# One-core chunk attention with a gated convolution: four single warming products, and the whole order of queues and buffers dealt anew

## The chip, the cores and the metric

The kernel runs on one NeuronCore of a Trainium2 chip. Five engines work side by side, each through its own queue in program order: TensorE (PE; its weight loads are listed as PEld), VectorE (DVE), ScalarE (ACT), GpSimd (POOL) and SyncE (SP), which here only issues DMAs. The metric is device microseconds of one execution; less is better. Before the change it is 277.35 us, the median of 3 runs (276.96 to 277.71).

## What is computed

```
scores = q @ k^T / 8 in chunks of 64 tokens;  attn = softmax(scores);  x = attn @ v      (8 batches x 8 heads x 576 x 64)
x as [8, 576, 512]:  gate = sigmoid(causal depthwise convolution of x with 5 taps);  val = x @ w_val
out = (gate * val) @ w_out
```

All of it is float32 for the caller. The kernel keeps that accuracy by splitting operands of the two large products in a high and a low part (`xh`, `xl`; `v_hi`, `v_lo`; `gh`, `gl`; `o_hi`, `o_lo`), so that each large product is three products of TensorE's faster 32-bit form: high by high, high by low, low by high. The weights come as 64-bit words and are cut into the two parts on the chip.

## The kernel before

The 4608 tokens are cut into nine groups of 512 (g = 0 to 8), each group's 512 channels into two halves (p = 0, 1). For a half there is a chain of pieces, each a handful of instructions:

- `lq`, `lk`, `lv` load queries, keys and values (512 KB each; those of group 0 partly in halves of 256 KB); `lw v c` and `lw o c` load a unit c of the two weight matrices, `lc` the taps.
- `S g p b` are the scores of a half (64x64 products on PE); `mx` finds the row maximum (DVE); then either `ng` and `ea` (exponentials on ACT with the sum read out, 16 times two instructions) and `rc`, or `sb` (DVE), `ex` (ACT), `sm` (DVE); `nm` scales by 1/sum (POOL).
- `T` or `TW` transposes (PE), `ec` copies the transposed weights out (ACT), `A g p` is attn @ v (PE); `xr`, `xd` and `xc` cut x into its high part, its low part and a plain copy (ACT, DVE, ACT); `hc` and `hb` keep the last tokens for the next group's convolution (POOL).
- `V g m c` is a product with w_val: three matmuls of 128x512, or one where a fourth number names the term. `vc` copies the sum out. `k0`, `k`, `kk`, `kx` are the convolution's taps (mostly DVE), `sg` the sigmoid, `gs` the gating product, `gr` and `gd` the cut of the result.
- `P g t c` is a product with w_out, `oc` (or `o1`) copies the sum out, `st` (or `s1`) stores it.
- `w1` to `w9`, `wa`, `wb`, `Q v c` and `wc` cut weight unit c; `W n s` is a stretch of n products of 128x512 and s of 128x64 on zeros, whose result nobody reads.

What runs when is written by hand: the string `ORDER` lists some 1030 pieces, and the loop at the end of the kernel function calls them one after the other. Each engine keeps that order in its queue, SP too. A capital D or G at a piece's end puts it on DVE or POOL. Three more tables set the rest. `SLOTS` names for every new tile the SBUF buffer (`z`, 28 whole ones and 10 in the tile `ys`), the PSUM bank (`b`, four of them) or the score buffer (`e`) that it takes. A tile that takes a buffer waits until its former tile's last reader is done; where that reader is a store, until the store has landed. `BEHIND` ties a piece on POOL to another piece that must have ended. A DMA issued from SP also takes one of eight completion counters in turn, and so waits for the DMA eight places before it.

Every instruction is recorded through one helper, so the profile gives nearly all of them one line (L144) and the tiles tell them apart:

```
def run(fn, *args, **kwargs):
    made.append(tc.keep_in_program_order(fn(*args, **kwargs)))
```

In the trace `z` and `ys` are the buffers of all kinds, `b` the banks, `e_row` the scores after the exponential, `mx` and `rs` the row maxima and sums, and `in_q`, `in_k`, `in_v`, `in_moe_w_val` and `in_moe_w_out` the inputs.

Of the kernel before, what the change touches and what calls it, by code (L numbers as in the profile page):

```python
# [22 lines left out]
rc 0 1 1,w6D v 3,sm 0 0,nm 0 1 1,ec 0 1 0,TW 0 1 1,Q v 3,lw v 0,lv 0 1,lv 0 0,lw o 0,lk 1 1,lq 1 1,w5 v 0,wc v 2,ec 0 1 1,wc v 3,
nm 0 0,w1 v 0,w4 c 0,mx 1 0,sb 1 0,A 0 1 1,A 0 1 0,TW 0 0,w2 v 0,xr 0 1 1,xr 0 1 0,xc 0 1 0,ec 0 0,ex 1 0,xc 0 1 1,V 0 3 2 0,
V 0 2 2 0,V 0 3 2 1,V 0 2 3 1,V 0 3 3 1,A 0 0,w3 v 0,w3 o 0,w1 o 0,w7 c 0,xd 0 1 0,w4 v 0,w8D c 0,w7 v 0,w9,sm 1 0,w6D v 0,
xd 0 1 1,w8 v 0,nm 1 0,wa v 0,xr 0 0,S 1 1 1,S 1 1 0,V 0 3 3 0,V 0 3 0 0,V 0 3 0 1,V 0 3 1 1,V 0 2 0 0,V 0 2 0 1,V 0 3 1 0,
V 0 2 1 1,V 0 2 3 0,V 0 2 1 0,T 1 0,lw o 3,lk 2 0,lv 1 0,lq 2 0,lv 1 1,lk 3 0,lw o 2,xc 0 0,k0 0 3,k0 0 2,k0 0 0,k0 0 1,ec 1 0,
xd 0 0,mx 1 1,k 0 3 2,ng 1 1,k 0 2 1,wbD v 0,w1 o 3,k 0 3 4,k 0 1 2,k 0 2 3,k 0 0 1,V 0 1 2 2,V 0 0 1 2,V 0 0 0 2,V 0 3 1 2,
V 0 3 2 2,V 0 0 2 0,V 0 1 3 1,V 0 0 3 0,V 0 3 3 2,V 0 0 2 2,V 0 2 1 2,V 0 1 1 2,V 0 0 1 0,V 0 1 0 2,V 0 1 3 2,V 0 2 0 2,V 0 2 2 2,
V 0 1 0 0,V 0 0 3 2,V 0 0 1 1,V 0 1 0 1,A 1 0,ea 1 1,w2 o 0,xr 1 0,xc 1 0,k 0 1 4,w3 o 3,rc 1 1,k 0 1 1,hc 0 1,nm 1 1,w1G o 2,  # L30
S 2 0 0,S 2 0 1,mx 2 0,xd 1 0,sb 2 0,V 0 1 2 1,V 0 2 2 1,V 0 3 0 2,V 0 0 3 1,V 0 1 2 0,V 0 1 1 1,V 0 1 3 0,V 0 0 2 1,V 0 1 1 0,
V 0 0 0 1,V 0 2 3 2,V 0 0 0 0,T 1 1,V 1 3 0,V 1 3 1,w2 o 3,w5 o 0,k0 1 1,w2 o 2,vc 0 0,ec 1 1,ex 2 0,lq 3 0,lq 2 1,lk 2 1,lk 4 1,
lw o 1,lv 2 1,lk 4 0,lq 3 1,lq 4 0,lv 2 0,lk 3 1,k 0 3 3,k 0 0 4,w4 o 0,k 1 1 3,w7 o 0,sm 2 0,A 1 1,S 2 1 1,S 2 1 0,vc 0 1,xc 1 1,
xr 1 1,mx 2 1,xd 1 1,ng 2 1,w8 o 0,nm 2 0,V 1 0 1,V 1 2 0,V 1 0 0,V 1 2 1,V 1 3 3,T 2 0,V 1 2 2,V 1 0 2,V 1 2 3,V 1 1 0,V 1 1 2,
V 1 1 1,w6 o 0,k0 1 3,w5 o 3,ea 2 1,ec 2 0,w4 o 3,k 0 0 2,w3 o 2,k 0 0 3,k 0 3 1,w3 o 1,k 0 2 4,k0D 1 2,k 0 2 2,k 1 1 1,w7 o 3,
rc 2 1,k 0 1 3,S 3 0 1,S 3 0 0,A 2 0,V 1 3 2,V 1 0 3,V 1 1 3,w1G o 1,nm 2 1,w8 o 3,sg 0 1,w6 o 3,xr 2 0,vc 1 1,sg 0 0,mx 3 0,
sb 3 0,xd 2 0,k 1 1 4,w4 o 2,waD o 3,gs 0 0,gs 0 1,k 1 2 4,TW 2 1,V 2 0 1,V 2 1 0,V 2 1 1,ec 2 1,xc 2 0,vc 1 0,w2 o 1,S 4 0 0,
A 2 1,xr 2 1,ex 3 0,xd 2 1,S 3 1 0,S 4 0 1,S 3 1 1,V 2 0 0,V 2 1 2,V 2 1 3,V 2 0 2,V 2 0 3,mx 4 0,sm 3 0,hc 0 0,wa o 0,wb o 0,
# [32 lines left out]
P 4 2 3,P 5 1 0,P 5 2 1,P 4 1 0,P 4 2 1,P 5 2 2,P 5 3 3,P 5 3 0,P 5 0 2,P 4 2 2,P 5 3 1,P 5 0 0,P 5 2 0,P 5 0 1,P 5 1 1,gr 6 1,
# [12 lines left out]
    z="21 1 24 27 13 25 9 12 26 3 21 6 7 10 24 8 5 18 19 14 4 8 27 22 3 9 24 23 10 13 7 15 6 11 8 27 17 15 10 14 0 "  # L84
# [660 lines left out]
```

## Time and profile before

| what | value |
|---|---|
| median of 3 runs | 277.35 us (276.96 to 277.71) |
| the profiled execution | 277.89 us, its span 276.1 us (1.8 us lie around the span) |
| PE busy | 265.8 us, 96% of the span |
| DVE, ACT, POOL busy | 236.5, 192.7 and 60.2 us |
| chain that ended last | 83% PE, 10% DMA, 2% DVE, 2% SP |
| granted TensorE clock, mean | 0.998 |
| moved by DMA | 42.48 MB; stores begin at 86 us, the last loads land near 151 us |

A busy matmul is counted to its modelled end, and matmuls overlap: in a dense stretch a product of 128x512 starts every 0.233 us (nine of them in the 2.10 us from 75.80 to 77.90), though one alone is listed with about 0.39 us. What counts on PE are therefore the starts, and the idle time in brackets before an instruction. DMAs leave SP in order and are served nearly in order; the time to landing is counted from the issue.

### The profile page before, as it was taken

How to read it: one execution, taken by the hardware profiler on the slowest of the kernel's cores; microseconds unless marked ns; L12 is line 12 of the kernel's file. 1: busy time of each engine (PE TensorE's matmuls, PEld its weight loads, DVE VectorE, ACT ScalarE, POOL GpSimd, SP SyncE). 2: the span in 40 equal slices, each digit the busy share in tenths (PEclk: the TensorE clock that was granted, in tenths of full speed). 3: DMA queues.
4: the chain of work that ended last, by engine and by line, in shares of the span. 5: the costliest groups of instructions: out<-in, count | busy, mean ns of one | idle time of the engine just before them, and what ended most of it. 6: DMA issues, size and time to landing. Idle time of an engine off the chain costs nothing.

```text
span 276.1 us, 8074 instructions
## 1 busy us (share of the span) xinstructions
PE 265.8 (96%) x3490; PEld 212.8 (77%) x3490; DVE 236.5 (86%) x316; ACT 192.7 (70%) x360; POOL 60.2 (22%) x59
## 2 busy tenths in 40 slices
...
PEclk9999999999999999999999999999999999999999
...
GB/s 241 391 373 221 285 350 363 303 3 182 409 26 158 374 223 271 53 331 204 5 233 229 2 2 2 0 0 2 0 0 1 2 0 0 0 0 61 265 379 209
DMA packets 14755, 42.48 MB, mean 154 GB/s; under 512 B 1536, under 2 KB 1792, under 8 KB 14720
## 3 DMA queue, kind: packets, MB, share of 16 engines
...
## 4 chain that ended last, share of the span: by engine, by line
PE 83%; DMA 10%; DVE 2%; SPq 2%; issue 1%; ACT 0%; DVEq 0%
PE b L144 83%; DMA z<-in_k 5%; DMA out<-z 3%; DMA z<-in_q 2%; SPq L144 2%; DVE e_row L144 1%; DVE mx L144 1%; DVE z L144 1%; ACT z L144 0%; DVEq L144 0%; ACT e_row L144 0%
## 5 line engine op out<-in xcount | busy, mean ns | idle before, releaser
L144 PE MATMUL b<-z,v_hi 128*128 128x512 f32 x288 | 93.9, 399 | 0.1
L144 PE MATMUL b<-o_hi,z 128*128 128x512 f32 (+1 forms) x296 | 93.9, 391 | 0.0
L144 ACT COPY z<-b 128x1024 f32<-128x1024 f32 (+2 forms) x63 | 59.7, 969 | 31.8 <-PE b L144 29.0
L144 PEld LDWEIGHTS b<-o_hi,z 128*128 128x128 f32 x296 | 55.1, 188 | 12.9 <-ACT e_row L144 0.2
L144 PEld LDWEIGHTS b<-z,v_hi 128*128 128x128 f32 x288 | 53.8, 188 | 13.2 <-issue 0.2
L144 DVE SCALAR_TENSOR_TENSOR z<-z,cw,z 128x509 f32<-128x509 f32 (+3 forms) x80 | 56.2, 739 | 1.9 <-ACT z L144 1.8
L144 PE MATMUL b<-o_lo,z 128*128 128x512 f32 (+1 forms) x148 | 57.5, 388 | 0.0
L144 PE MATMUL b<-z,v_lo 128*128 128x512 f32 x144 | 56.2, 396 | 0.0
L144 POOL TENSOR_TENSOR z<-e_row,rs 128x1024 f32<-128x1024 f32 (+1 forms) x17 | 31.5, 1856 | 46.7 <-DVE rs L144 33.4
L144 POOL TENSOR_TENSOR z<-z,z 128x1024 fp32r<-128x1024 f32 (+2 forms) x8 | 14.7, 1843 | 118.3 <-ACT z L144 101.0
L144 PEld LDWEIGHTS b<-o_lo,z 128*128 128x128 f32 x148 | 27.8, 188 | 6.0
L144 ACT ACTIVATE z<-z 128x1024 f32<-128x1024 f32 (+3 forms) x26 | 21.4, 843 | 14.9 <-DVE z L144 14.4
L144 DVE SCALAR_TENSOR_TENSOR ys<-ys,cw 128x509 f32<-128x509 f32 (+7 forms) x32 | 31.0, 1010 | 1.0 <-ACT ys L144 0.9
L144 PEld LDWEIGHTS b<-z,v_lo 128*128 128x128 f32 x144 | 27.0, 188 | 6.0
L144 DVE TENSOR_TENSOR z<-z,z 128x1024 f32<-128x1024 f32 (+2 forms) x22 | 25.4, 1170 | 5.1 <-ACT z L144 5.0
L144 ACT ACTIVATE e_row<-b,mx 128x64 f32<-128x64 f32 x80 | 23.8, 362 | 3.0 <-DVE mx L144 3.0
L144 DVE TENSOR_TENSOR z<-b,z 128x1024 fp32r<-128x1024 f32 (+1 forms) x19 | 21.7, 1161 | 2.3 <-ACT z L144 1.1
L144 DVE TENSOR_REDUCE mx<-b 128x16 f32<-128x1024 f32 (+1 forms) x19 | 21.7, 1142 | 1.9 <-PE b L144 1.9
L144 PEld LDWEIGHTS b<-z,z 64*64 64x64 f32 x1024 | 16.6, 135 | 8.2 <-issue 5.0
L144 PE MATMUL b<-z,z 64*64 64x64 f32 x1024 | 18.5, 221 | 4.4 <-DMA z<-in_k 3.9
L144 ACT CAST z<-b 128x1024 fp32r<-128x1024 f32 (+1 forms) x19 | 18.2, 976 | 6.1 <-PE b L144 6.0
L144 ACT ACTIVATION_READ_ACCUMULATOR e_row<-b,mx 128x1 f32 x80 | 20.3, 256 | 0.0
...
## 6 DMA issues: line engine op xcount, KB each, us to landing
out<-z SPq DMA_DIRECT2D x16, 512.0 KB, 5.1
z<-in_k SPq DMA_DIRECT2D x9, 512.0 KB, 4.4
z<-in_v SPq DMA_DIRECT2D x9, 512.0 KB, 7.9
ys<-in_v SPq DMA_DIRECT2D x9, 512.0 KB, 6.2
z<-in_q SPq DMA_DIRECT2D x8, 512.0 KB, 6.1
ys<-in_q SPq DMA_DIRECT2D x8, 512.0 KB, 7.7
ys<-in_k SPq DMA_DIRECT2D x7, 512.0 KB, 5.5
z<-in_moe_w_val SPq DMA_DIRECT2D x4, 512.0 KB, 5.2
```

The lines of the kernel that those rows point to most:

```text
L144: made.append(tc.keep_in_program_order(fn(*args, **kwargs)))
```

## The change

`ORDER` has the same 1030 pieces and four more: `W 1 1`, `W 1 3`, `W 1 4` and `W 1 2`, together 4 products of 128x512 and 10 of 128x64. The stretch `W 3`, which opened PE's queue, moves to a place between the scores of group 0, and `W 1 1` opens it. Everything else in `ORDER`, all buffer and bank numbers, and the ties of POOL (24 before, 27 now) are written anew. No function changes, and no other instruction is added or removed. At the front, `lv 0 1` is now issued ahead of `lw v 0`. One stretch of the diff, where the first result of the group 0 goes out (the rest of the table reads alike):

```
-V 3 0 2,V 3 1 2,V 3 0 0,V 3 3 0,P 0 1 3,V 3 1 1,V 3 3 3,V 3 3 2,V 3 2 2,V 3 2 1,V 3 3 1,ea 5 1,sg 1 0,oc 0 0,sg 1 1,gs 1 0,
+P 0 0 1,P 0 1 2,P 0 0 2,V 3 2 2,V 3 1 0,V 3 0 3,V 3 3 0,V 3 2 3,V 3 1 3,V 3 3 2,V 3 0 2,V 3 1 1,ea 5 1,oc 0 0,sg 1 0,sg 1 1,
```

The first place is PE's queue at the front, from the second weight unit's sum (three products into bank 3) to the third's. Before, the scores of group 1 (`b0_293`, 32 products) follow the first transposes (`b2_288`):

```order
L144 MATMUL b0_207<-z6_181,z21_179 64x64 x32
L144 MATMUL b3_279<-z12_102,ident_62 128x512
L144 MATMUL b3_279<-v_hi_67,signed_63 128x512
L144 MATMUL b3_279<-z26_109,signed_63 128x512
L144 MATMUL b2_288<-ident_62,z8_283 128x128 x4
L144 MATMUL b0_293<-z24_252,z10_250 64x64 x32
L144 MATMUL b2_288<-ident_62,z8_283 128x128 x4
L144 MATMUL b1_339<-z3_111,ident_62 128x512
```

And now, the same stretch of PE's queue without the products before the weight unit's sum:

```order
L146 MATMUL b3_283<-z10_104,ident_62 128x512
L146 MATMUL b3_283<-v_hi_67,signed_63 128x512
L146 MATMUL b3_283<-z16_109,signed_63 128x512
L146 MATMUL b2_300<-ident_62,z24_287 128x128 x4
L146 LDWEIGHTS warm_64
L146 MATMUL b1_305<-warm_64 128x512
L146 LDWEIGHTS warm_64
L146 MATMUL b1_305<-warm_64 128x64
L146 LDWEIGHTS warm_64
L146 MATMUL b1_305<-warm_64 128x64
L146 MATMUL b0_309<-z17_247,z11_245 64x64 x32
L146 MATMUL b2_300<-ident_62,z24_287 128x128 x4
```

`W 1 2` now stands between the first transposes and the scores of group 1, and takes bank 1, which the scores of group 0's other half had.

The second place is SP's queue around the first stores. Before, one store (`st 0 1`) stands there, and the values of group 4's half 0 (`lv 4 0`, into `z11_1662`) follow it directly in a buffer that a weight unit had:

```order
L144 DMA z14_1659<-in_q 128x1024
L144 DMA out_0<-z25_1522 128x2x512
L144 DMA z11_1662<-in_v 128x1024
L144 DMA ys_61<-in_k 128x1024
L144 DMA ys_61<-in_v 128x1024
L144 DMA ys_61<-in_q 128x1024
```

And now, the same stretch of SP's queue:

```order
L146 DMA z15_1676<-in_q 128x1024
L146 DMA out_0<-z16_1545 128x2x512
L146 DMA ys_61<-in_k 128x1024
L146 DMA ys_61<-in_v 128x1024
L146 DMA ys_61<-in_k 128x1024 x2
L146 DMA out_0<-z11_1667 128x2x512
L146 DMA z11_1684<-in_v 128x1024
L146 DMA ys_61<-in_q 128x1024
```

A second store (`st 0 0`, out of `z11_1667`, the tile that `oc 0 0` fills) now stands ahead of `lv 4 0`, and `lv 4 0` goes into the same buffer 11.

The third place is SP's queue at its last loads, those of values for groups 6 to 8. Before, `lv 6 1` (`z9_1972`) stands ahead of three stores of groups 0 and 2:

```order
L144 DMA ys_61<-in_q 128x1024
L144 DMA z9_1972<-in_v 128x1024
L144 DMA ys_61<-in_v 128x1024
L144 DMA out_0<-z17_2381 128x2x512
L144 DMA out_0<-z27_1652 128x2x512
L144 DMA z26_2395<-in_v 128x1024
L144 DMA ys_61<-in_v 128x1024
L144 DMA out_0<-z14_2170 128x2x512
```

And now, the same stretch of SP's queue:

```order
L146 DMA out_0<-z14_2188 128x2x512
L146 DMA ys_61<-in_v 128x1024 x2
L146 DMA out_0<-z16_2297 128x2x512
L146 DMA out_0<-z6_1973 128x2x512
L146 DMA z6_2410<-in_v 128x1024
L146 DMA ys_61<-in_v 128x1024
L146 DMA z20_2413<-in_v 128x1024
```

`lv 6 1` (`z6_2410`) now stands behind three stores, `st 2 0`, `st 2 1` (out of `z16_2297`, which `oc 2 1` fills) and `st 1 0` (out of `z6_1973`), and goes into the buffer of the last of them.

## Rows read from the trace of the kernel before

**Rows 1.** The page: busy time of each engine; PE's granted clock in 40 slices

```profile
PE 265.8 (96%) x3490; PEld 212.8 (77%) x3490; DVE 236.5 (86%) x316; ACT 192.7 (70%) x360; POOL 60.2 (22%) x59
...
PEclk9999999999999999999999999999999999999999
```

**Rows 2.** Timeline of PE at the front: start, length, instruction [idle before, releaser]

```profile
9.63 1.46 PE L144 MATMUL b<-z,z 64*64 64x64 f32 x64 [1.33 <-DMA z<-in_k]
...
11.74 0.69 PE L144 MATMUL b<-z,z 64*64 64x64 f32 x32 [0.65 <-DMA z<-in_k]
...
22.25 1.09 PE L144 MATMUL b<-ident,z 128*128 128x128 f32 x8 [0.64 <-POOL z L144]
26.06 1.16 PE L144 MATMUL b<-z,z 64*64 64x64 f32 x64 [0.45 <-DMA z<-in_q]
```

**Rows 3.** Timeline of PE from 143 to 158 us: its last waits on DVE

```profile
153.55 0.71 PE L144 MATMUL b<-ident,z 64*128 64x64 f32 x16 [0.22 <-DVE z L144]
...
154.69 0.72 PE L144 MATMUL b<-ident,ys 64*128 64x64 f32 x16 [0.42 <-DVE z L144]
```

**Rows 4.** Two stretches: length; PE, PEld, DVE, ACT, POOL; clock, DMA share, GB/s

```profile
12.00:22.00 10.00, 7.54 (x207) 5.13 (x197) 8.92 (x18) 9.04 (x39) 5.03 (x4) 1.00 0.97 374
80.00:100.00 20.00, 20.00 (x233) 16.38 (x232) 19.38 (x28) 17.81 (x48) 4.48 (x3) 1.00 0.55 191
```

**Rows 5.** Timeline of PE around one and around two groups of 64 small products

```profile
75.80 0.63 PE L144 MATMUL b<-o_hi,z 128*128 128x512 f32 x2
...
77.90 0.40 PE L144 MATMUL b<-o_hi,z 128*128 128x512 f32 x1
...
79.66 0.39 PE L144 MATMUL b<-o_lo,z 128*128 128x512 f32 x1
...
146.55 0.39 PE L144 MATMUL b<-z,v_hi 128*128 128x512 f32 x1
...
149.23 0.39 PE L144 MATMUL b<-z,v_lo 128*128 128x512 f32 x1
```

**Rows 6.** Timeline of DVE and ACT at the front

```profile
14.21 1.17 DVE L144 TENSOR_REDUCE mx<-b 128x16 f32<-128x1024 f32 x1
...
18.62 0.67 ACT L144 ACTIVATE z<-z 128x512 f32<-128x512 uint32 x1 [0.41 <-DMA z<-in_moe_w_val]
```

**Rows 7.** DMA issued at 11.5 us: KB each, median us to landing

```profile
z<-in_moe_w_val SPq DMA_DIRECT2D x1, 512.0 KB, 7.1
```

**Rows 8.** DMA queues from 13 to 16 us: packets, MB, share of 16 engines

```profile
q8 instruction: 1, 0.02, 2.3%
```

**Rows 9.** Timeline of DVE from 82 to 92 us

```profile
82.02 1.22 DVE L144 TENSOR_TENSOR z<-b,z 128x1024 fp32r<-128x1024 f32 x1 [0.48 <-ACT z L144]
83.16 2.72 DVE L144 SCALAR_TENSOR_TENSOR z<-z,cw,z 128x511 f32<-128x511 f32 x4
...
91.42 0.17 DVE L144 TENSOR_SCALAR mx<-mx 128x16 f32<-128x16 f32 x1
```

**Rows 10.** Timeline of ACT from 91 to 97 us: first and last of 32 instructions

```profile
91.62 0.31 ACT L144 ACTIVATE e_row<-b,mx 128x64 f32<-128x64 f32 x1 [2.04 <-DVE mx L144]
...
96.17 0.29 ACT L144 ACTIVATION_READ_ACCUMULATOR e_row<-b,mx 128x1 f32 x1
```

**Rows 11.** Timeline of ACT from 138 to 141 us: the copy ahead of a store

```profile
139.07 1.00 ACT L144 COPY z<-b 128x1024 f32<-128x1024 f32 x1
```

**Rows 12.** DMA issued at 253.39 us, with no other in flight: KB, us to landing

```profile
out<-z SPq DMA_DIRECT2D x1, 512.0 KB, 3.0
```

**Rows 13.** DMA issued at 98.37 us, with no other in flight

```profile
z<-in_k SPq DMA_DIRECT2D x1, 512.0 KB, 3.3
```

**Rows 14.** Timeline of PE: 16 transposes, then A 4 0

```profile
102.46 0.71 PE L144 MATMUL b<-ident,z 64*128 64x64 f32 x16
103.10 1.16 PE L144 MATMUL b<-z,z 64*64 64x64 f32 x64
```

**Rows 15.** DMAs issued at 140.09 and 140.54 us, behind a load

```profile
out<-z SPq DMA_DIRECT2D x2, 512.0 KB, 5.9
```

More of the change, by code (lines that the diff above doesn't have):

```diff
@@ L23 @@
[L23 to L38, printed above, removed]
@@ L79 @@
[L79 to L84 removed]
[6 rows of a table removed]
[L91 to L92 removed]
+ORDER = """zr 1,zr 0,zw,zi,zs 0,zs 1,lw v 1,lk 0 1 0,lw v 2,lw v 3,lq 0 1 0,lq 0 1 1,lk 0 1 1,w1 v 1,w3 v 1,w2 v 1,w5 v 1,w4 v 1,w7 v 1,
@@ new lines @@
+w5 v 0,ec 0 1 1,nm 0 0,w1 v 0,mx 1 0,sb 1 0,w3 v 0,w3 o 0,w1 o 0,w4 c 0,w7 c 0,A 0 1 1,A 0 1 0,TW 0 0,w2 v 0,wc v 3,xc 0 1 1,
+xc 0 1 0,xr 0 1 1,xr 0 1 0,ec 0 0,ex 1 0,V 0 2 3 1,V 0 2 3 0,V 0 3 2 1,V 0 3 3 1,V 0 2 2 1,A 0 0,xd 0 1 0,w4 v 0,w6D v 0,w8D c 0,
+w7 v 0,sm 1 0,w9,xd 0 1 1,w8 v 0,nm 1 0,wa v 0,w2 o 0,xr 0 0,xc 0 0,k0 0 0,k0 0 2,k0 0 3,k0 0 1,V 0 2 2 2,V 0 2 2 0,S 1 1 1,
+V 0 2 0 1,V 0 3 0 0,V 0 2 0 0,V 0 3 2 2,V 0 3 0 1,V 0 2 1 0,V 0 3 2 0,V 0 3 3 2,S 1 1 0,T 1 0,lv 2 0,lw o 3,lv 1 0,lq 2 0,lk 2 0,
@@ new lines @@
+lv 1 1,lk 4 0,lw o 2,ec 1 0,xd 0 0,k 0 0 1,mx 1 1,ng 1 1,wbD v 0,w4 o 0,k 0 2 1,k 0 3 2,w1 o 3,k 0 3 4,k 0 1 2,V 0 1 2 2,
+V 0 0 3 2,V 0 1 3 0,V 0 3 3 0,V 0 1 2 0,V 0 2 3 2,V 0 1 1 1,V 0 2 1 2,V 0 3 0 2,V 0 0 3 1,V 0 0 1 2,V 0 0 2 1,V 0 1 3 2,V 0 2 0 2,
+V 0 0 3 0,V 0 1 0 1,V 0 1 2 1,V 0 3 1 1,V 0 0 1 0,V 0 3 1 2,V 0 0 0 0,V 0 1 1 2,A 1 0,ea 1 1,w2 o 3,w6 o 0,xr 1 0,xc 1 0,k 0 2 3,
+k 0 1 4,k 0 0 4,rc 1 1,w3 o 3,nm 1 1,w1G o 2,S 2 0 1,S 2 0 0,V 0 2 1 1,V 0 1 1 0,V 0 0 1 1,V 0 1 0 0,V 0 0 0 2,V 0 3 1 0,
@@ new lines @@
+V 0 1 3 1,V 0 1 0 2,V 0 0 2 2,V 0 0 0 1,V 0 0 2 0,mx 2 0,xd 1 0,sb 2 0,T 1 1,k0 1 1,vc 0 1,vc 0 0,ec 1 1,ex 2 0,w2 o 2,w5 o 0,
+lk 2 1,lq 2 1,lq 3 1,lv 2 1,lq 4 0,lw o 1,lk 3 1,lq 3 0,lk 3 0,k 1 1 3,w7 o 0,w3 o 2,k 0 1 1,k 0 3 3,sm 2 0,V 1 1 0,V 1 3 1,
+V 1 2 0,A 1 1,S 2 1 0,S 2 1 1,xr 1 1,xc 1 1,k0 1 3,w5 o 3,mx 2 1,xd 1 1,ng 2 1,w8 o 0,nm 2 0,V 1 0 1,V 1 2 1,V 1 0 0,V 1 3 3,
+V 1 2 3,V 1 0 2,V 1 1 1,V 1 3 2,T 2 0,V 1 0 3,V 1 3 0,ea 2 1,ec 2 0,k 0 0 2,k 0 1 3,k 1 1 1,k 0 2 4,w4 o 2,k 0 3 1,w7 o 2,w4 o 3,
@@ new lines @@
+k 0 2 2,rc 2 1,w7 o 3,k 0 0 3,S 3 0 1,S 3 0 0,V 1 2 2,A 2 0,w1G o 1,hc 0 1,nm 2 1,w8 o 3,hc 0 0,sg 0 0,vc 1 1,xr 2 0,sg 0 1,
+w6 o 3,mx 3 0,sb 3 0,k 1 1 4,xd 2 0,k0D 1 2,waD o 3,gs 0 1,w58 o 2,k 1 2 4,gs 0 0,V 1 1 2,V 1 1 3,TW 2 1,V 2 0 1,V 2 0 0,V 2 1 0,
+ec 2 1,vc 1 0,xc 2 0,w6 o 2,A 2 1,xr 2 1,ex 3 0,xd 2 1,S 3 1 1,S 4 0 0,S 4 0 1,S 3 1 0,V 2 1 1,V 2 1 3,V 2 1 2,V 2 0 3,V 2 0 2,
+mx 4 0,sm 3 0,wb o 3,wa o 0,wb o 0,hc 1 0,nm 3 0,xc 2 1,gr 0 1,gr 0 0,vc 2 0,w2 o 1,mx 3 1,sb 4 0,ng 3 1,gdD 0 1,waD o 2,w3 o 1,
@@ new lines @@
+T 4 1,A 4 0,S 5 0 0,S 5 0 1,ec 4 1,vc 3 0,gr 1 1,k 2 3 3,gdD 1 0,rc 5 1,k 2 2 2,k 2 0 4,mx 5 0,sb 5 0,k 2 0 1,k 2 1 2,k 2 0 2,
+A 4 1,hc 2 1,gd 1 1,hc 3 0,xr 4 1,xc 4 0,xc 4 1,xr 4 0,sg 2 0,sg 2 1,xd 4 0,xd 4 1,gs 2 1,gs 2 0,nmD 5 1,P 1 3 1,P 1 2 1,P 1 3 0,
+P 1 2 0,P 1 2 3,P 1 2 2,P 1 3 3,P 1 1 0,P 1 1 2,P 1 3 2,P 1 1 1,P 1 1 3,S 6 1 0,S 6 1 1,S 6 0 1,S 6 0 0,P 1 0 0,P 1 0 2,P 1 0 1,
+P 1 0 3,ex 5 0,gr 2 0,gr 2 1,oc 1 1,oc 1 0,lv 5 1,lk 7 0,lq 7 0,lk 8 1,lk 7 1,lq 8 1,st 1 1,lk 8 0,lq 7 1,lv 5 0,sm 5 0,mx 6 0,
@@ new lines @@
+mx 6 1,sb 6 0,gd 2 0,nm 5 0,gd 2 1,sb 6 1,ex 6 0,sm 6 0,P 2 1 0,P 2 1 1,P 2 0 1,T 5 1,T 5 0,ec 5 1,ex 6 1,ec 5 0,S 7 0 0,S 7 0 1,
+A 5 1,mx 7 0,sm 6 1,nm 6 0,nm 6 1,xc 5 1,xr 5 1,sb 7 0,xd 5 1,P 2 0 2,P 2 1 2,P 2 2 3,P 2 0 3,P 2 1 3,P 2 2 2,T 6 1,P 2 2 0,
+P 2 0 0,ex 7 0,ec 6 1,kx 4 3,k0 4 1,oc 2 0,S 8 0 0,S 7 1 0,S 8 0 1,S 7 1 1,P 2 3 0,P 2 3 2,P 2 3 1,P 2 3 3,P 2 2 1,T 6 0,sm 7 0,
+kk 4 3 3,nm 7 0,ec 6 0,oc 2 1,mx 8 0,sb 8 0,mx 7 1,sb 7 1,kk 4 3 2,k 4 1 1,T 7 0,A 5 0,S 8 1 0,S 8 1 1,ec 7 0,ex 7 1,xr 5 0,
@@ new lines @@
+xc 5 0,k0 5 0,k0 4 0,ex 8 0,sm 7 1,st 2 0,lv 7 0,lv 8 1,st 2 1,st 1 0,lv 6 1,lv 8 0,lv 7 1,nm 7 1,xd 5 0,mx 8 1,sb 8 1,ex 8 1,
+k 4 1 2,sm 8 0,sm 8 1,k 4 0 3,V 4 0 3,V 4 2 1,V 4 1 3,V 4 1 1,V 4 3 1,V 4 2 0,V 4 2 2,V 4 1 0,V 4 1 2,A 7 0,A 6 1,V 4 0 2,V 4 3 3,
+V 4 3 2,V 4 0 0,V 4 0 1,V 4 2 3,V 4 3 0,xc 6 1,xr 6 1,xr 7 0,xc 7 0,vc 4 0,vc 4 1,nm 8 1,nm 8 0,xd 6 1,A 6 0,T 8 1,T 8 0,ec 8 1,
+xr 6 0,xc 6 0,xd 7 0,k 4 1 4,k 4 0 1,kk 4 3 1,k0D 5 1,k 5 1 3,ecD 8 0,k 4 0 4,xd 6 0,V 5 1 2,V 5 1 0,V 5 0 3,V 5 0 1,V 5 3 2,
@@ new lines @@
+V 5 3 1,V 5 2 0,V 5 2 1,A 8 0,T 7 1,V 5 2 3,V 5 0 0,xc 8 0,xr 8 0,ec 7 1,k 5 1 2,k 5 1 1,kxD 4 2,k 4 1 3,xd 8 0,kk 4 2 4,k 4 0 2,
+kk 4 2 1,kk 4 3 4,V 5 3 3,V 5 3 0,V 5 2 2,V 5 0 2,A 7 1,A 8 1,V 5 1 3,V 5 1 1,vc 5 1,xr 7 1,xc 7 1,xc 8 1,xr 8 1,kx 6 3,vc 5 0,
+sg 4 0,kx 6 2,xd 7 1,kk 4 2 2,xd 8 1,k 5 0 3,k 5 0 1,k0D 3 2,kk 4 2 3,k 5 0 4,k 5 0 2,kk 6 2 2,k 3 2 1,gs 4 0,V 7 1 0,V 7 1 1,
+V 7 1 2,V 7 0 2,V 7 2 2,V 7 2 0,V 7 0 3,V 6 0 3,V 6 2 2,V 6 3 2,V 7 3 1,V 6 1 2,V 6 0 0,V 7 1 3,V 6 2 3,V 6 2 1,V 6 0 1,V 6 1 0,
@@ new lines @@
+V 6 3 1,V 7 0 0,V 7 3 0,V 7 2 1,V 6 1 1,V 7 0 1,V 6 0 2,V 6 1 3,V 7 3 2,V 6 3 0,V 7 3 3,V 7 2 3,V 6 3 3,V 6 2 0,hc 4 1,hc 4 0,
+hc 6 0,hc 6 1,hc 5 0,hc 3 1,hc 7 0,hb 0,hc 7 1,hc 5 1,hb 1,sg 5 1,kx 6 0,gr 4 0,sg 4 1,kx 6 1,kk 6 2 4,gs 5 1,gs 4 1,gdD 4 0,
+kk 6 0 3,kk 6 3 2,kk 6 1 3,kk 6 0 4,k 5 1 4,gr 5 1,k0 3 3,k0 8 0,vc 6 0,vc 7 0,vc 6 1,gr 4 1,k0 3 0,vc 7 1,k0 8 1,sg 5 0,k0D 8 2,
+kk 6 1 4,kk 6 0 1,gdD 4 1,k 3 3 1,kk 6 2 3,k 3 3 4,kk 6 1 2,kk 6 3 4,gdD 5 1,k 8 0 1,kk 6 2 1,k 3 3 2,kk 6 0 2,kk 6 1 1,gs 5 0,
@@ new lines @@
+k 8 1 2,kk 6 3 1,kk 6 3 3,V 8 3 1,V 8 3 0,V 8 1 3,V 8 3 3,V 8 1 2,V 8 2 2,V 8 3 2,V 8 1 1,P 4 0 1,V 8 1 0,V 8 0 0,V 8 2 3,V 8 0 3,
+V 8 0 2,P 4 1 1,P 4 0 0,V 8 0 1,P 4 3 0,P 4 1 3,V 8 2 0,V 8 2 1,P 4 0 2,P 4 1 0,P 4 3 1,P 4 0 3,sg 7 0,vc 8 1,k0 3 1,vc 8 0,
+gr 5 0,sg 7 1,sg 6 0,sg 6 1,gdD 5 0,gs 7 1,k 3 0 4,k 8 0 4,k 3 3 3,k 3 1 3,gs 6 0,k 8 0 2,k0D 8 3,gs 6 1,k 3 0 3,k 8 1 3,k 3 1 2,
+k 3 1 4,gs 7 0,P 5 0 2,P 4 2 0,P 5 0 3,P 4 2 3,P 4 3 2,P 5 1 2,P 5 2 3,P 5 3 3,P 5 3 0,P 5 1 3,P 5 0 0,P 4 2 2,P 4 1 2,P 5 1 0,
```

72 lines of the change are left out of this document (25 added, 47 removed), and 23 rows, old and new, of tables (BEHIND, z).

## The prediction, made before the changed kernel was run

> **What bounds the kernel now.** [...] So PE sets the time, and the change can win only from its waits, or lose by making new ones. The timeline of PE tells where they are. At the front there are six, from 9.63 us (1.33 idle) to 26.06 us (0.45), together 5.0 us; four wait for keys, one for POOL, one for queries [rows 2]. After that PE runs dense until two small waits on DVE at 153.55 and 154.69, 0.22 and 0.42 [rows 3], and dense again to the tail, whose pieces keep their order. Recoverable are thus about 5.0 us at the front and 0.64 us late.
>
> The table of stretches says what stands behind PE. From 12 to 22 us DVE is busy for 8.92 of 10 us, ACT for 9.04, and the DMA engines for 0.97 of the time: three resources are full beside PE's waits. From 80 to 100 us PE is full and DVE has only 0.62 us free in 20 [rows 4]. What DVE loses there it cannot give back.
>
> All terms below stand against the profiled execution, 277.89 us (span 276.1 and 1.8 around it). That is 0.54 above the median of 277.35, so 0.54 comes off at the end. A difference within 0.3%, 0.83 us, is about what a measurement of this kernel cannot tell from none.
>
> **The change part by part.**
>
> *The four W stretches.* They add 4 products of 128x512 and 10 narrow ones. At the dense spacing, 2.10 us for nine from 75.80 to 77.90 [rows 5], the wide ones cost 0.93 if nothing covers them; spread over the front's 5.0 us of waits they cost nothing. The clock has nothing to gain, since it is granted in full there already [rows 1, 4]. I take 0; W 1 2 takes the bank of the scores of the other half, but the scores behind it would wait for their data as long.
>
> *The front.* For group 0's second half the queries come last, not keys, and its first scores start earlier by about the 0.65 that the second wait for keys takes [rows 2]. But the same DVE and ACT work follows [rows 4], and the order puts one more row maximum of 1.17 us [rows 6] ahead of the reciprocal that the first transposes need. So these come no earlier. On SP `lv 0 1` now goes ahead of `lw v 0`. Before, that load left at 11.5 us and took 7.1 [rows 7]: landed at 18.6, where ACT's first cut of it began after 0.41 us of waiting, at 18.62 [rows 6]. With 512 KB more ahead, at 374 GB/s [rows 4], it lands 1.4 later, at 20.0. ACT waits there, and the copy of the transposed weights stands behind that cut. That is at worst 1.0 us late for PE (1.4 less the 0.41 that ACT had waited). At best the keys' 0.65 carries on, less one crossing of 0.37 (below): -0.3. I take the middle, +0.3.
>
> One more thing bears on this load. In its 7.1 us an instruction packet took 2.3% of the DMA engines' time between 13 and 16 us [rows 8], which is 0.023 x 3.0 x 16 = 1.1 us of one engine. The 28 extra PE instructions ahead of group 1's scores move such a packet forward. If it had held the load back, the load now lands at 18.9 and the front's term falls to -0.1. [...]
>
> *Crossings.* Each time PE goes from 128x512 products to small ones and back it loses time. One group of 64 takes 1.76 us from the last wide product to the second one after it (77.90 to 79.66), two groups in a row 2.68 (146.55 to 149.23) [rows 5]. So a group is 0.92, and a crossing 1.76 - 0.92 - 2 x 0.233 = 0.37. Of the order of the pieces I count 20 such stretches before and 24 now, the front's two among them; some transposes now stand beside scores or attention and save about 0.2. The net is +0.9 ahead of A 4 0 and +0.2 behind it.
>
> *A 4 0 and the first stores.* Here the change adds a wait. `lv 4 0` is behind `st 0 0` in SP's queue, and in its buffer. So it follows this chain. DVE's max of group 5 (91.42) comes later by one more tap, 2.72 / 4 = 0.68, less the 0.48 for which DVE had idled at 82.02: +0.2 [rows 9]. ACT's 32 instructions end at 96.17 + 0.29 = 96.46 before [rows 10], 96.66 now. `oc 0 0` directly behind takes 1.00, as such a copy does [rows 11], to 97.7. The store leaves at 97.75 and lands after 3.0 if alone [rows 12], at 100.75; the load takes 3.3 if alone [rows 13], and with 0.1 to start the product it is 104.15. A 4 0 started at 103.10 [rows 14]. So it is 1.05 late, and 0.2 more for DVE's own lag: +1.3. Between ends: 0.7 if DVE's tap costs nothing and ACT keeps its time, and 4.2 if the store takes the 5.9 of a pair behind a load [rows 15] instead of 3.0. The nearest row is the one alone, as nothing else is ready to leave then. Everything later on PE queues behind A 4 0, and DVE's cut of x behind that. The front and the crossings before it, 0.3 + 0.9 = 1.2, are inside this 1.3, not added.
>
> *A 6 1 and three stores.* `lv 6 1` is now behind `st 2 0`, `st 2 1` and `st 1 0`, and in the buffer of the last. From the end of `T 6 0` (call it t), ACT copies `ec 6 0` and `oc 2 1`, 1.00 each [rows 11], so `st 2 1` leaves at t + 2.0. If stores follow at once, `st 1 0` lands 3.0 [rows 12] and 512 KB more (1.3) later, t + 6.3, and `lv 6 1` 3.3 + 0.1 on, t + 9.7. With 5.9 for a pair [rows 15] plus the 0.45 between its issues it is t + 11.75. PE has, ahead of A 6 1, transposes of 0.64 [rows 14], 27 wide products of 0.233 (6.3), three groups of 0.92 and its half crossings: t + 10.0. The wait is between 0 and 1.8. I take +0.9, the middle; V of group 4 stands behind it on PE, so it is all on the path.
>
> *The two late waits* on DVE [rows 3] go with a cut of x that was held by a store's buffer: -0.64.
>
> **Sum.** 1.3 + 0.9 - 0.64 + 0.2 = +1.76; 277.89 + 1.76 = 279.65, less 0.54 is 279.1. I say 279.0.
>
> **The rivals.**
>
> *No change* (0.24). The buffers of the two chains come free in time: `lv 4 0` is hidden by PE's own lateness and `lv 6 1` costs nothing. Then the front at -0.3, the crossings at +0.9 + 0.2 and the late waits at -0.64 remain: +0.1, 277.5. For it speaks that the chains miss by only 1.05 and 0.9 us; against it that DVE is full from 80 us on [rows 4].
>
> *Faster* (0.14). The earlier scores carry through, -0.65, the late waits are gone, -0.64, and half of the crossings' 1.1 hides in waits: -0.7, which is 276.6; with all of it hidden 276.0. It needs a DVE and an ACT with room from 12 to 22 us, which the row denies, and neither of the two store waits. It decides once A 4 0 starts no later than before.
>
> *Slower by more* (0.11). The store ahead of `lv 4 0` takes the 5.9 us of a pair: 2.9 more at A 4 0, 282.0. Stores of this kernel do take that behind a load; at this place none stands ahead. It decides from a landing 4 us after the issue on.
>
> The forecast has 0.51, with its own range of 278.2 to 280.2 (A 4 0 from 0.7 up, A 6 1 from 0 to 1.8). Of the rivals, half of *faster* and most of *slower by more* lie outside 276.5 to 280.9, which leaves 8 in 10 and some within. Faster by more than 0.83: 0.14. Within: 0.24. Slower: 0.51 + 0.11 = 0.62.
>
> **What would show it.** In the profile of the changed kernel PE waits for values (in_v) near 104 us, about 1 us, and again near 148; if neither wait is there, the two largest terms fall and with them the sign. ACT waits for the value weights (in_moe_w_val) near 19 to 20 us. No wait on DVE near 153. The wide gaps around small products are 24 with 0.37 us each. A landing of `st 0 0` much over 3 us would make it the slowest case, and transposes that start before their 22.25 of now [rows 2] the fastest. If PE's granted clock falls below 9 anywhere, none of these terms explains the time.

## The result: 281.32 us against 277.25, slower by 1.5%

The changed kernel took 281.32 us (median of 4 runs, 280.42 to 282.60), the kernel before 277.25 us beside it (4 runs, 276.96 to 277.71): a ratio of 1.0149, 95% interval 1.0102 to 1.0196. That is 4.1 us more. The prediction was 279.0, 1.75 us more, in a range of 276.5 to 280.9: the sign was right, but the change forecast was less than half of the one measured, and 281.32 lies above the range. A second set of 5 runs gave 281.59 (281.06 to 282.89). The nine runs of the changed kernel lie 2.5 us apart; those of the kernel before lay up to 3.9 us apart beside the experiments below (276.02 to 279.95 over 23 runs), so its scatter is not larger. Some runs below took over 1.5% longer than the fastest of the same kernel, four of seven of them in one experiment (f1) at a lower granted clock (0.971 to 0.988), and the ratios leave these out.

The profiled execution took 280.73 us, span 278.9, against 277.89 and 276.1 before: +2.84. That is less than 4.1, because the profile of before lies 0.64 above its median of 277.25, and this one 0.59 below 281.32. The page, to lay beside [rows 1]:

```profile
PE 268.7 (96%) x3504; PEld 213.8 (77%) x3504; DVE 238.8 (86%) x316; ACT 193.6 (69%) x360; POOL 61.1 (22%) x59
...
PEclk9999999999999999999999999999999999999999
```

The shares have not moved and the clock is granted in full (9 in every slice, 1.0 in the mean). PE's busy time has grown by 2.9 us and its idle time has not, but busy is counted to modelled ends; so the loss is read from where PE's starts fall behind. PE's timeline at the front of the changed kernel (start, length, instruction, idle before and releaser):

```profile
17.00 0.66 PE L146 MATMUL b<-ident,z 128*128 128x128 f32 x4 [1.01 <-POOL z L146]
17.50 0.44 PE L146 MATMUL b<-warm 128*128 128x512 bf16 x3
17.86 0.69 PE L146 MATMUL b<-z,z 64*64 64x64 f32 x31
19.47 0.70 PE L146 MATMUL b<-z,z 64*64 64x64 f32 x33 [0.92 <-issue]
```

Two waits are to be seen. The transposes wait for POOL, whose `nm 0 1 0` came late behind the moved row maximum, as forecast. The other one was not in the forecast: the 64 products of group 1's scores break off after 31 and go on 0.92 us later, released by "issue", which is nothing that the profile shows. Same inputs, same bank, no semaphore between the 31st and the 32nd. Further on (the transposes of group 0's other half, A 0 0, a row of 128 products, then T 4 1 and A 4 0, then A 6 1):

```profile
23.81 1.09 PE L146 MATMUL b<-ident,z 128*128 128x128 f32 x8 [0.64 <-POOL z L146]
...
26.00 1.16 PE L146 MATMUL b<-z,z 64*64 64x64 f32 x64
...
37.21 2.46 PE L146 MATMUL b<-z,z 64*64 64x64 f32 x128
...
104.20 0.71 PE L146 MATMUL b<-ident,z 64*128 64x64 f32 x16
105.70 1.16 PE L146 MATMUL b<-z,z 64*64 64x64 f32 x64 [0.79 <-DMA z<-in_v]
...
151.34 1.16 PE L146 MATMUL b<-z,z 64*64 64x64 f32 x64 [0.77 <-DMA z<-in_v]
```

Against [rows 2] the first is 1.56 late (23.81 for 22.25), T 4 1 is 1.74 late and A 4 0 2.60 [rows 14]. A 6 1 waits 0.77, and no wait on DVE is left near 154 [rows 3]. So 1.56 + 0.18 + 0.86 + 0.77 - 0.64 = 2.73 of the 2.84.

ACT's first cut of `lw v 0`, against [rows 6]:

```profile
20.03 0.69 ACT L146 ACTIVATE z<-z 128x512 f32<-128x512 uint32 x1 [1.01 <-DMA z<-in_moe_w_val]
```

It is at 20.03, and the landing had been put at 20.0. The chain to A 4 0: ACT's first exponential, the copy behind the last, then (from the DMA table, for what was issued at 99.41 and 102.27) KB and us to landing of the store and of `lv 4 0`:

```profile
93.61 0.32 ACT L146 ACTIVATE e_row<-b,mx 128x64 f32<-128x64 f32 x1 [2.09 <-DVE mx L146]
...
98.27 1.11 ACT L146 COPY z<-b 128x1024 f32<-128x1024 f32 x1
```

```profile
out<-z SPq DMA_DIRECT2D x1, 512.0 KB, 2.8
```

```profile
z<-in_v SPq DMA_DIRECT2D x1, 512.0 KB, 3.3
```

Every link is within about 0.2 us of the length that was worked out for it; only its start was 1.8 later than the 91.82 of the sum (91.62 and the 0.2 of a tap).

### The profile page after: what moved, and what is told of

It reads as the page before. It is cut to its first block, busy times and chain, and to the rows that moved or that the text cites. A ratio compares the mean times of both kernels' runs of the same rounds, so it can differ in the third digit from the quotient of the medians.

```text
span 278.9 us, 8096 instructions
## 1 busy us (share of the span) xinstructions
PE 268.7 (96%) x3504; PEld 213.8 (77%) x3504; DVE 238.8 (86%) x316; ACT 193.6 (69%) x360; POOL 61.1 (22%) x59
## 4 chain that ended last, share of the span: by engine, by line
PE 80%; DMA 8%; DVE 4%; ACT 3%; SPq 2%; issue 1%; POOL 1%; ACTq 0%; POOLq 0%
PE b L146 80%; DVE z L146 3%; DMA z<-in_k 3%; DMA out<-z 3%; DMA z<-in_v 3%; ACT e_row L146 2%; SPq L146 2%; ACT z L146 1%; POOL z L146 1%; DVE mx L146 1%; DVE rs L146 1%; ACTq L146 0%; POOLq L146 0%
## 5 line engine op out<-in xcount | busy, mean ns | idle before, releaser
L146 DVE SCALAR_TENSOR_TENSOR z<-z,cw,z 128x508 f32<-128x508 f32 (+3 forms) x80 | 56.8, 742 | 0.2
L146 POOL TENSOR_TENSOR z<-e_row,rs 128x1024 f32<-128x1024 f32 (+1 forms) x17 | 30.9, 1816 | 52.2 <-DVE rs L146 37.5
L146 POOL TENSOR_TENSOR z<-z,z 128x1024 fp32r<-128x1024 f32 (+2 forms) x8 | 15.4, 1919 | 113.4 <-ACT z L146 98.6
L146 PE MATMUL b<-z,z 64*64 64x64 f32 x1024 | 19.2, 221 | 4.4 <-DMA z<-in_v 1.6
L146 ACT ACTIVATION_READ_ACCUMULATOR e_row<-b,mx 128x1 f32 x80 | 19.4, 242 | 0.0
```

## The experiments

Each time is a median, each ratio is to the kernel before, measured beside it. "A" is the changed kernel, "B" the one before; the label in brackets is the name by which an experiment is spoken of further on.

**The change again** (ctl). A, unedited.

> The changed kernel again, beside the others on one chip. All theories: 280.4 to 282.6 us as in its four runs, ratio to before 1.011 to 1.019. What is looked at is how far its own runs and its front differ: if the wait in the middle of group 1's scores, which the trace puts down to no other engine (0.92 us near 19 us), is there again with another length, it is a property of the front and not of one execution.

281.59, ratio 1.0165 (1.0135 to 1.0195). The wait inside the scores was not there in this profile (PE came to them later, at 18.86); 0.77 and 0.69 us for in_v were, and the transposes came at 24.18, A 0 0 at 26.35. So the waits for values belong to the order; the break in the scores comes and goes, and the front is as late without it.

**Without the four W stretches** (a1).

```
-W 1 1,W 9 22 ... S 0 1 0,W 1 3 ... W 1 4,Q v 2 ... TW 0 1 0,W 1 2,
+W 9 22 ... S 0 1 0 ... Q v 2 ... TW 0 1 0,
```

> The changed kernel without its four single W stretches (14 products whose result nobody reads); all else in its order. Theory 1, the 28 extra PE instructions bring a page of PE's instructions due before it has come: the 0.92 us wait without a releaser near 19 us is gone, the front's lateness falls from 1.56 to about 0.5 (ACT's wait for the value weights is then last), total 1.0 less, 280.3. Theory 2, the page is late because it is queued behind data loads, whatever PE has done: a wait without a releaser of 0.5 to 0.9 us is still there some 14 products later, and the total falls by 0.2 at most, 281.1. Theory 3, the W stretches themselves hold PE: the total falls by what they take beyond the waits, 0.3.

283.26, ratio 1.0198 (1.0161 to 1.0236): not faster, and none of the three. The wait near 19 us is gone, as it also was in A's second profile, but one of 1.64 us has come 127 us later, in a row of small products that the edit does not touch:

```profile
142.82 1.64 PE L153 MATMUL b<-z,ys 64*64 64x64 f32 x100
146.10 0.46 PE L153 MATMUL b<-z,ys 64*64 64x64 f32 x16 [1.64 <-issue]
```

That led to a count. Number PE's records in order (weight loads, products, semaphores): this wait stands at number 5057, the one of the result at 449. In twelve profiles of experiments and changed kernel (f1 left out) there are some 20 places where, inside a row of equal products and with no data to wait for, the next start is about 0.3 us or more off, and all stand, within two records, at 449 plus a multiple of 256. The page gives q8, the instruction queue, 27 packets of 0.44 MB: 16 KB each, one for some 260 of PE's 7,000 instructions. At each of these places, by the trace's single records, PE goes on 1.33 to 1.59 us after an instruction packet has ended. That PE waits there for its own program is the author's reading of this; the trace shows the place, the packet and the time. The 256 instructions from one such number to the next are called a page of instructions, or a page, below.

**`lv 4 0` ahead of `st 0 0`, in buffer 12** (a3).

```
-lk 6 0,st 0 0,lv 4 0,      (lv 4 0 in buffer 11)
+lk 6 0,lv 4 0,st 0 0,      (lv 4 0 in buffer 12)
```

> The changed kernel with lv 4 0 in a buffer that is free (12) and ahead of st 0 0 in SP's queue. Theory 1: PE's wait for in_v near 105 us (0.79 us) is gone, the time falls by 0.8, 280.5. Rival: DVE is full there and its lateness comes back as a wait on DVE or ACT before 125 us; the time stays at 281.3.

280.71, ratio 1.0129 (1.0090 to 1.0168). The wait at A 4 0 is gone, but 0.64 of the 0.79 is taken back at A 6 1. ACT's copy and the first of the two stores ahead of `lv 6 1` did come earlier with PE, by 0.96 us, but the two stores took longer to land here (4.7 us in the median, 4.0 in the result's profile):

```profile
104.73 1.16 PE L153 MATMUL b<-z,z 64*64 64x64 f32 x64
...
151.02 1.16 PE L153 MATMUL b<-z,z 64*64 64x64 f32 x64 [1.41 <-DMA z<-in_v]
```

**`lv 6 1` ahead of the stores, in buffer 9** (a4).

```
-st 2 0,lv 7 0,lv 8 1,st 2 1,st 1 0,lv 6 1,      (buffer 6)
+lv 6 1,st 2 0,lv 7 0,lv 8 1,st 2 1,st 1 0,      (buffer 9)
```

> The changed kernel with lv 6 1 in a free buffer (9) and ahead of the three stores in SP's queue. Theory 1: PE's wait for in_v near 151 us (0.77 us) is gone, the time falls by 0.8, 280.5. Rival: what follows waits on DVE's cut of x instead, as in the kernel before (0.64 us near 154 us), and 0.1 to 0.2 is all that is won, 281.1.

280.82, ratio 1.0130 (1.0084 to 1.0176). PE's wait at A 6 1 is gone and A 4 0's stays (0.72). The time lies between theory 1 and its rival, and its interval overlaps that of A: that the wait is gone the profile shows, not the time.

**Both** (a34).

> The changed kernel with both value loads set free: lv 4 0 (buffer 12, ahead of st 0 0) and lv 6 1 (buffer 9, ahead of the stores). In the run with lv 4 0 alone the wait at A 6 1 grew from 0.77 to 1.41 us, so A 6 1 was held by its store chain to a time of its own. Theory 1: with both gone the two gains add, neither wait for in_v is left, and the time falls by 1.6 from 281.5 to 279.9. Rival: the next waits behind A 6 1 take it, on DVE's cut of x near 154 to 160 us; 280.9.

279.63, ratio 1.0069 (1.0036 to 1.0102): 2.0 less than A by the medians, 2.7 by the ratios (A's second set, whose interval does not overlap). Theory 1 had 279.9. Neither wait for in_v is left; what is, in its profile, is one for keys, of `lk 2 0` behind `lq 2 0`:

```profile
39.42 1.16 PE L153 MATMUL b<-z,z 64*64 64x64 f32 x64 [1.39 <-DMA z<-in_k]
```

**And `lq 2 0` in a free buffer**, 5 for 11 (d1).

> The changed kernel with lv 4 0 and lv 6 1 set free, and lq 2 0 in a free buffer (5) as well, so that it and lk 2 0 behind it no longer wait on SP for the scores of group 1. In the runs of this order PE waited for lk 2 0 near 39 us for between 0 and 1.4 us. Theory 1: that wait is gone, and the time falls from 279.63 to 279.0. Rival: the loads brought forward push the values or weights behind them, 279.6.

279.36, ratio 1.0079 (1.0047 to 1.0111): that wait is gone from the profile, and the time is the same within its interval.

**The front's two edits undone**, in A (a29): `rc 0 1 0` ahead of `mx 0 0`, `lw v 0` ahead of `lv 0 1`.

```
-mx 0 0,rc 0 1 0,   ... lv 0 1,lw v 0,   "nm 0 1 0": "mx 0 0"
+rc 0 1 0,mx 0 0,   ... lw v 0,lv 0 1,   "nm 0 1 0": "rc 0 1 0"
```

> The changed kernel with two edits at the front: the reciprocal rc 0 1 0 goes ahead of the row maximum mx 0 0 on DVE again (and nm 0 1 0 on POOL is tied to it), and lw v 0 is issued ahead of lv 0 1 again. Theory 1: the front's lateness (A 0 0 at 25.3 to 26.4 us in the four profiles of this front, 24.45 before) comes from POOL's late nm 0 1 0 (PE waits 1.0 us for POOL at the first transposes) and, close behind, from ACT's late cut of lw v 0; with both undone A 0 0 starts at 24.4 to 24.9 and the time is 280.4 against 281.5. Theory 2, PE's own instructions come late in the middle of the scores of group 1 whatever DVE does: a wait without a releaser is still there and A 0 0 stays past 25.3; 281.3.

282.26, ratio 1.0185 (1.0141 to 1.0228): no gain. POOL's wait at the first transposes is gone, but `W 1 2` behind them waits 0.50 for its bank, number 449 stops the scores until 18.85, and 705 stops PE for 0.97 at 26.7. At A 6 1 PE is 3.2 us later than in the result's profile and waits no less:

```profile
154.56 1.16 PE L153 MATMUL b<-z,z 64*64 64x64 f32 x64 [1.01 <-DMA z<-in_v]
```

**`lv 0 1` ahead of `lw v 0`, in B** (b2).

```
-lw v 0,lv 0 1,
+lv 0 1,lw v 0,
```

> The kernel before with one edit: lv 0 1 is issued ahead of lw v 0, as the changed kernel has it. Theory 1: lw v 0 lands 1.3 us later, ACT's first cut of it is at 19.9 instead of 18.62, the copy behind it holds A 0 1 1 (20.45 before) until 21.3, the front is 0.5 to 0.9 late and so is the end: 278.0 against 277.36. Rival, the front has room on ACT for it: no change, 277.4.

277.41 against 277.28, ratio 1.0010 (0.9984 to 1.0035): this part of the change costs nothing that can be measured, and the time of theory 1 falls. In its one profile the front is late even so (A 0 0 at 25.49), with a break at 449:

```profile
17.32 1.16 PE L152 MATMUL b<-z,z 64*64 64x64 f32 x45
19.09 0.56 PE L152 MATMUL b<-z,z 64*64 64x64 f32 x19 [0.61 <-issue]
```

**The four W stretches alone, in B**, in banks that are free there (b1).

> The kernel before with the four W stretches put in at the places that the change gives them (W 1 1 first, W 1 3 behind S 0 1 0, W 1 4 ahead of Q v 2, W 1 2 behind TW 0 1 0), in banks that are free there. Theory 1: they lie in waits and cost nothing by themselves; as page 449 had 1.1 us of room there and the boundary moves by 14 products of 0.014 us, no new wait: 277.3. Rival: they hold PE back or move a page boundary into a dense row: 278.

276.89 against 276.78, ratio 0.9994 (0.9960 to 1.0029). They cost nothing, as forecast. From the transposes of group 0's other half to T 4 1 no wait of PE is listed in its profile:

```profile
21.96 1.09 PE L152 MATMUL b<-ident,z 128*128 128x128 f32 x8 [0.63 <-POOL z L152]
...
101.42 0.71 PE L152 MATMUL b<-ident,z 64*128 64x64 f32 x16
```

**More and fewer products in the opening stretch of A** (d2).

```
-W 9 22        (A)
+W 5 60        (d2_more: 34 products more, about as long)
+W 12          (d2_less: 19 fewer)
```

> The changed kernel with its opening stretch W 9 22 (9 wide, 22 narrow products) made W 5 60, which takes about as long and has 34 products more. In all profiles so far a wait without a releaser inside a row of small products stands where PE's instruction number is 449 + a multiple of 256, and ends 1.35 to 1.45 us after an instruction packet of 16 KB has come. Theory 1 (pages of 256 PE instructions, asked for one page ahead and queued behind data): the page for number 449 is asked for 34 products earlier, in the first scores near 9.5 instead of 10.7 us, comes by 17, and is needed ahead of the scores of group 1: no wait inside those scores, total 0.4 to 0.9 less than 281.5. Theory 2 (the wait belongs to the scores of group 1, their data or their bank): it is there as before, 281.5.

> The changed kernel with W 9 22 made W 12, 19 products fewer. Theory 1: the page for instruction 449 is asked for later, behind the wait for group 0's other keys at 12.9 us, comes at about 19 and is usable at 20.5; PE waits 1.2 to 1.7 us without a releaser near the end of group 1's scores, total 0.3 to 0.8 more than 281.5. Theory 2: the wait stays at the same product of group 1's scores and of the same size, 281.5.

283.79 (1.0248, 1.0171 to 1.0325) and 283.22 (1.0210, 1.0139 to 1.0281). Both medians are above A's, but the intervals overlap with A's. The positions went as theory 1 has it; its time for more products (0.4 to 0.9 less) did not. With more, the scores at the front run through, and new waits stand at 2497 and 3777, the first between two wide products just behind rows of small ones:

```profile
18.47 1.16 PE L153 MATMUL b<-z,z 64*64 64x64 f32 x64
...
68.45 0.50 PE L153 MATMUL b<-z,v_lo 128*128 128x512 f32 x1 [1.06 <-issue]
...
111.19 0.38 PE L153 MATMUL b<-z,ys 64*64 64x64 f32 x9 [1.17 <-issue]
```

With fewer, the break in the scores moves 19 products on, to the last 14, and one stands at 5057, where it also stood without the W stretches:

```profile
18.86 0.46 PE L153 MATMUL b<-z,z 64*64 64x64 f32 x14 [0.36 <-issue]
...
143.86 0.44 PE L153 MATMUL b<-z,ys 64*64 64x64 f32 x11 [1.56 <-issue]
```

Theory 1 failed in the size at 449 (0.36, not 1.2 to 1.7): the packet had come at 17.4, 0.6 us earlier than in the result's profile, though PE went into the page before it 1.8 us later (12.5 for 10.7). In the longer opening PE went into it at 9.6, and the packet had come at 13.0. So when PE gets there does not set it alone. That a packet is asked for one page ahead, or stands behind data, was the author's theory and is not shown.

**22 narrow products fewer in B**, nothing else (f1).

```
-W 3,W 9 22,
+W 3,W 9,
```

> The kernel before with its opening stretch W 9 22 made W 9: 22 narrow products of no use fewer, everything else the same. Theory 1 (a page of 256 instructions is asked for one page ahead and takes some 2.6 us to come and 1.4 to be usable, while PE runs through 256 instructions of small products in 1.84 us): all later page boundaries lie 22 products further on, and worked out from the starts of the trace of before, numbers 2241 (63 us), 3521 (105 us) and some of 1217, 4289 and 6081 now fall into the middle of rows of small products: waits without a releaser of 1 to 2 us at two to four of these places, time 279 to 282 against 276.8. Theory 2, such waits belong to the changed order: 276.8.

Ratio 1.0128 (1.0080 to 1.0175) over three runs: a kernel with less work is 3.5 us slower (0.0128 x 277.3). In its profile, of which only the places are read, PE breaks off at 1217, 2241, 3521 and 4289, four of the five numbers named before the run (not at 6081), and at 1473 and 5313. Whether the shorter opening cost granted clock as well (0.993 to 1.0 in the mean of the three) was not separated.

**The changed order at the best page position**: d1 with `W 9 31` for `W 9 22` (f2).

> The changed kernel with lv 4 0, lv 6 1 and lq 2 0 set free, and 9 narrow products more in the opening stretch (W 9 31). Theory 1: worked out from the starts in the trace of the version without the 9, no page boundary behind the front is then in a row of small products with less than 4.0 us since the last; the waits without a releaser near 64 and 141 us are gone, the one near 18 us stays (0.7 to 1.0 us). Time 278.5 against 279.36. Theory 2: no change, 279.4.

279.17, ratio 1.0076 (1.0053 to 1.0099), and 278.85 to 279.76 over six runs where d1 had 278.08 to 281.38 over twelve. No break is left in its profile, not even the one near 18 us that was expected to stay; the median is the same. That the breaks made the scatter is not shown: B's runs scatter too, without a break in its profiles. The expected 278.5 was not reached, and A 0 0 is at 26.56 in its profile, 24.44 in B's first.

**And the front's two edits undone there** (g1).

> The version with lv 4 0, lv 6 1 and lq 2 0 set free and W 9 31, and at the front rc 0 1 0 ahead of mx 0 0 on DVE and lw v 0 ahead of lv 0 1 on SP, as before the change. Theory 1: PE's wait for POOL at the first transposes (1.0 us) is gone and A 0 0 starts 0.8 to 1.2 us earlier than without these two edits; 278.2 against 279.17. Theory 2: the front is held by something else (the bank of W 1 2, ACT), 279.2.

279.73, ratio 1.0074 (1.0042 to 1.0106). No gain again: the transposes are 1.9 us earlier (16.09 for 17.98), but `W 1 2` behind them waits for its bank, which DVE still reads, the scores then for page 449, and A 0 0 is at 25.99:

```profile
16.09 0.66 PE L153 MATMUL b<-ident,z 128*128 128x128 f32 x4
17.25 0.43 PE L153 MATMUL b<-warm 128*128 128x512 bf16 x3 [0.50 <-DVE e_row L153]
17.61 0.57 PE L153 MATMUL b<-z,z 64*64 64x64 f32 x22
18.88 0.85 PE L153 MATMUL b<-z,z 64*64 64x64 f32 x42 [0.70 <-issue]
```

**B's late waits on DVE, by another buffer** (c1: `xd 6 1` in 16 for 14), **and by an earlier store** (c2: `st 2 0` ahead of `lv 7 1`).

> The kernel before with one edit: xd 6 1 takes buffer 16, which is free, in place of 14, which the store st 2 0 holds. DVE's wait for out (0.69 us near 152 us) goes, and PE's waits of 0.22 and 0.42 us behind it. Theory 1: PE is dense from there to the tail, so 0.6 is won: 276.7 against 277.36. Rival: the end is set by DVE there, which gives nothing back: 277.3.

> The kernel before with st 2 0 issued ahead of lv 7 1 and lv 8 1, about 2 us earlier, so that DVE's xd 6 1 (which takes its buffer, and waited 0.69 us for it to land) need not wait, with no buffer changed. Theory 1: PE's waits of 0.22 and 0.42 us near 154 us go, the time falls by 0.4 to 0.6 from 276.8. Rival: nothing to be measured, 276.8.

279.77 (1.0085, 1.0055 to 1.0115) and 276.98 (0.9999, 0.9977 to 1.0021). In both the waits near 154 are gone. The first is slower because buffer 16 now stays taken until the last product of V 6, and ACT's next copy into it waits for PE, then PE for DVE:

```profile
189.15 1.02 ACT L152 COPY z<-b 128x1024 f32<-128x1024 f32 x1 [6.71 <-PE b L152]
```

```profile
203.36 0.72 PE L152 MATMUL b<-o_hi,z 128*128 128x512 f32 x2 [1.45 <-DVE z L152]
```

By the second the two waits are worth no more than 0.64 us (0.0023 x 277), which is no less than what the prediction gave them.

**B for a second profile.**

> The kernel before, for a second profile of it. Theory 1: no wait without a releaser inside a row of small products, as in the first profile; 276.0 to 278.1 us. Rival, such waits come and go in every order: one or two of 0.3 us or more.

276.23 in one run, and no break at any page. With the first profile, c1 and c2 that makes four of B's order without one. The waits on DVE near 154 and the one for queries at 26.06 [rows 2] [rows 3] are not in this profile either, though nothing was edited: they belonged to the first execution. No version here beats B by more than its interval.

## Why the prediction was right in sign and wrong in size

Two steps failed. The first is the overlap at A 4 0: the prediction held the front and the crossings (0.3 + 0.9) to be inside the 1.3 us of A 4 0, and the runs show them added to it. The second is the size of the front, +0.3 at most +1.0, where 1.56 was measured. Term by term, profile against profile:

- *The W stretches cost 0.* Right for the products as such: put into B they change nothing (0.9994). But each product is also two instructions (3504 products and 3504 weight loads in the profile), and moves every later page boundary (with 19 fewer, in d2, the break in the scores came 19 products later); that was weighed only as a load that might be held up, not as a stop of PE itself. And the bank of `W 1 2`, put at nothing, is the next wait once POOL's is gone (0.50 in a29 and g1).
- *The front, +0.3 between -0.3 and +1.0.* It was +1.56, beyond both ends. Its two links were there (POOL later, `lw v 0` cut at 20.03). The instruction packet weighed beside that load began at 17.04 us for 14.46 before, so it did not come earlier, and the load landed at 20.0 and not at 18.9. In this profile the 0.92 us at number 449 came on top, but A's second profile is 1.93 late at the same transposes (24.18) without it. So the term was too small either way, and which link sets it stays open. What the traces show of the pages is their stops: 0.92 us here, 1.17 to 1.64 in three experiments.
- *Crossings, +0.9 ahead of A 4 0 and +0.2 behind.* Between 23.81 and T 4 1 only 0.18 more was measured (1.74 - 1.56), but the profile of before has waits of its own there, 0.45 for queries among them [rows 2]. In b1 no wait is listed in this stretch, and it takes 79.46 us (21.96 to 101.42). The changed kernel takes 80.39 for the same products, of which 0.36 is a short stop in the row at 37.21 (2.46 us, 2.10 for that row before). About +0.6 is left, for 15 rows of small products among the wide ones where there were 13. Behind T 4 1 it is 169.41 us to the last product in b1 and 169.61 in d1, +0.2 as forecast. So the kind of cost was right and the first size somewhat high. (The prediction's own count, four at 0.37 less 0.2, gives 1.3 and not 1.1.)
- *A 4 0, +1.3 in all, with the front and the crossings inside it.* Here the sum went wrong. The wait was 0.79, near the 1.05 that its links give (the 0.2 of DVE's tap is in the 1.05 already and was added once more), but it came on top of the 1.74. The chain to `lv 4 0` starts with DVE and ACT work that follows PE: from ACT's first exponential to T 4 1 it is 10.59 us in both profiles of A and 10.60 in a4, at 93.61, 94.05 and 95.33. So it was late with PE, and the sum had set a time from before, 104.15, against a PE that had moved. Adding gives 1.74 + 0.86 = 2.60. The prediction's own terms, added, would have made 0.3 + 0.9 + 1.3 + 0.9 - 0.64 + 0.2 = 2.96 for the 2.84 of the profiles; that it comes so near is partly luck, as the front was larger and other terms smaller.
- *A 6 1, +0.9.* Right: 0.77. This chain starts from PE too, with ACT's copies behind T 6 0, and so earlier lateness of PE does not hide it: in a29 PE comes there 3.2 us later and still waits 1.01. Lateness that arises behind its start does: in a1 and in the shorter opening of d2, breaks of 1.64 and 1.56 stand between T 6 0 and A 6 1, and no wait for values is left there. Why it grew to 1.41 in a3, by longer stores, one profile cannot tell. Freed together, the two loads win 2.0 us (a34).
- *The late waits, -0.64.* They are not in the changed kernel, but neither are they in B's second profile: the term was read from one execution. c2 could not tell their worth from none.
- *The rivals.* "Slower by more" came nearest by its time, but not by its place: the store ahead of `lv 4 0` took 2.8 us, not 5.9.

So of some 4.2 us (281.5 against 277.3), 2.0 are the two value loads behind stores (shown by a34). About 2 stay with the value loads, `lq 2 0` and the pages mended (279.17). Some 0.8 of these are the crossings, by the profiles above; no run takes them away alone. The rest agrees with the front: A 0 0 starts at 24.2 to 24.5 us in the profiles of B's order (b2 and f1 aside) and at 25.2 to 27.0 in those of A's. Which part of the front it is was not settled; undoing its two plain edits (a29, g1) did not win it back. What the pages take of the 4.2 is open as well: that a shift of instructions can cost time is clear of noise in B alone (f1).
